# A gated scan with a router and eight experts: a new order for the last dozen units, seven of them gated by GpSimd and TensorE, two copies on VectorE, three fills held back

## The chip, the cores and the metric

The kernel runs on one core of one Trainium2 chip, as one launch. The metric is the device time of that launch in microseconds (us). The engines are TensorE (PE, and PEld for its weight loads), VectorE (DVE), ScalarE (ACT), GpSimd (POOL) and SyncE (SP), which here issues nearly all the transfers from one queue in the order of the program.

## The reference

All tensors are float32. A gated linear recurrence runs over 4 sequences of 5,056 tokens with 256 channels, and its output, as 20,224 tokens, goes to a mixture of 8 experts with one expert for each token and a capacity of 80.

```
log_a = 8 * sigmoid(r_gate) * log(clip(sigmoid(a_param)))
a_t   = exp(log_a);  norm = sqrt(max(1 - a_t*a_t, 1e-6))
x_g   = norm * sigmoid(i_gate) * x
h     = a_t * h + x_g          # one step for each token; y[t] = h
logits = y @ w_gate (256 x 8);  expert = argmax;  gate = its softmax
for each expert e (w1: 256 x 1024, w2: 1024 x 256):
    keep the 80 tokens with the highest gate
    out[kept] = gate * (relu(y[kept] @ w1[e]) @ w2[e])
every other row of out is 0
```

Only 640 of 20,224 rows of the output are not zero, so nearly the whole output is a fill with zeros.

## The kernel before, in words

**Units.** The tokens are cut into 40 units of 512 (the last has 256). For each unit three tiles of 512 KB are loaded (`Lr`, `Li`, `Lx`, line 120). The r gate is transposed by TensorE (`Tr`, line 128: eight matmuls of 128x128), ScalarE takes its tanh out of PSUM (`tr`, line 130) and the decay from it (`e`, line 142), GpSimd squares the decay (`q`, line 145) and ScalarE takes the root (`s`, line 148). ScalarE takes the tanh of the i gate (`ti`, line 152). The product (1 + tanh i) * x is made either on VectorE in one instruction (`v`, line 159) or on GpSimd in two (`u`, lines 156 and 157: add one, then multiply). TensorE transposes that product, half a unit at a time (`Tu`, line 164: four matmuls), VectorE multiplies it with the root in PSUM (`xg`, line 167) and runs the recurrence (`y`, line 175), both once for each half of the channels.

**Router.** After every four units TensorE makes logits (`G`, line 238); the steps `R0` to `R5`, with ten stages each, turn them into gates. Stage 0 copies 128x512 logits from PSUM (line 262, ScalarE), stages 2, 4 and 6 are VectorE's, stage 5 and 7 GpSimd's. After the last unit stand the rest of step 5, the merge (`M`) of the candidates, and a stretch of small instructions that picks 80 tokens for each expert (lines 484 to 539).

**Fills.** Row blocks of 512 tokens of the output are set to zero by SP (`Z`, line 230), 40 of them; all but the first are copied from the part of the output that is already zero (512 KB read, 512 KB written). They stand between the loads.

**Experts.** Each expert has a pair of halves. In a half, TensorE runs eight groups of two matmuls for the first product of expert e+1 and two for the second product of expert e (lines 629 and 631). When a half has been issued, SP loads that half's weights of the expert two further on (`load_w1`, line 381, and `load_w2`, line 384; 512 KB each) into the buffer just read. The first two experts' weights are loaded before (`W0` to `W7`), into slots of the big tile that the last units leave. GpSimd, ScalarE and VectorE gather the tokens' columns (lines 616 and 617). An indirect transfer on GpSimd's queue (line 649) writes the result of an expert to the output, and it may not run before the fills have landed.

**What sets the order.** `ORDER` is a list of tokens as named above, written out by hand or by a program. Each engine gets its instructions in this order, and SP its transfers. `SLOTS` says which of 50 slots of 512 KB holds each tile of each unit; a load waits until the slot's last reader is done, and everything behind it on SP's queue waits with it.

Of the kernel before, what the change touches and what calls it, by code (L numbers as in the profile page):

```python
# [13 lines left out]
ALU = mybir.AluOpType  # L14
# [14 lines left out]
SLOTS = dict(r=(14, 25, 30, 35, 38, 18, 21, 16, 34, 9, 11, 20, 13, 26, 25, 37, 42, 45, 40, 48, 41, 49, 22, 31, 24, 30, 44, 45, 41, 46, 49, 35, 32, 37, 42, 46, 44, 45, 41, 46),  # L29
             i=(34, 40, 4, 27, 37, 44, 23, 37, 28, 19, 15, 23, 32, 18, 46, 49, 38, 16, 21, 30, 28, 25, 26, 34, 37, 32, 43, 36, 38, 31, 36, 30, 41, 45, 36, 43, 49, 37, 38, 49),  # L30
             x=(20, 12, 29, 22, 40, 24, 6, 42, 36, 29, 27, 35, 41, 24, 36, 17, 29, 18, 27, 43, 33, 38, 47, 42, 33, 28, 32, 27, 34, 38, 33, 34, 48, 33, 38, 48, 40, 43, 40, 47),
             a=(15, 8, 31, 19, 33, 5, 14, 7, 17, 10, 30, 12, 28, 34, 14, 23, 35, 38, 19, 20, 27, 35, 23, 29, 25, 26, 40, 47, 28, 29, 43, 31, 40, 47, 34, 35, 36, 42, 48, 39))
# [32 lines left out]
    R5.4 Z R5.5 R5.6 R5.7 R5.8 F F F F F F F F M2 R5.9  # L65
"""
EARLY = 8


class Plan:  # L70

# [12 lines left out]
def moe_kernel(ctx, tc, x, r_gate, i_gate, a_param, w_gate, w1, w2, out, capacity=80):  # L84
# [75 lines left out]
    def u_transposes(u, h):  # L160
        pu = pus[u, h] = ps_u.tile([P, C], F32, name="pu")
        nb = ntok(u) // P
        for b in range(nb):
            nc.tensor.transpose(pu[:, b:nb * P:nb], tmb('x', u)[:, b, h * P:(h + 1) * P], ident)  # L164
# [556 lines left out]
```

## Time and profile before

| | |
|---|---|
| three runs | 292.08, 293.74 and 287.35 us, median 292.08 us |
| profiled execution | 287.59 us, of which the span is 285.9 us |
| busy: DVE, ACT, POOL, PE | 223.0, 232.9, 213.0, 211.1 us |
| moved by DMA | 100.74 MB, mean 352 GB/s |

The span runs from the first to the last instruction that the profiler recorded. Busy time is the time in which an engine had an instruction in work. Up to about 201 us the units run, to about 218 us the last router step and the picking of tokens, and then the experts.

### The profile page before, as it was taken

Reading aid. Unit: us, or ns where it says so; the run is one execution under the profiler, and the core shown is the slowest. Engines: PE = TensorE matmul, PEld = TensorE weight load, DVE = VectorE, ACT = ScalarE, POOL = GpSimd, SP = SyncE. Lnnn points to the kernel's source line nnn. Section 1 sums busy time; section 2 is a strip of 40 time slices with the busy share of each in tenths; the row PEclk is TensorE's granted clock in tenths of the full one; section 3 lists DMA queues with packets and bytes.
Section 4 is the critical chain, followed back from the end, with each engine's and each line's share of the span. In section 5 each row is a group of like instructions: output and inputs, shape, how many; then the busy total and the mean of one; then the engine's idle time right before and its main releaser. Section 6 shows DMA issues by size and latency. Waiting matters only on the chain.

```text
span 285.9 us, 5799 instructions
## 1 busy us (share of the span) xinstructions
PE 211.1 (74%) x1488; PEld 161.0 (56%) x1488; DVE 223.0 (78%) x506; ACT 232.9 (81%) x488; POOL 213.0 (75%) x372
## 2 busy tenths in 40 slices
PE   2635849598556985479857696486787889999995
PEld 2634723375444354462555325333676779999994
DVE  2018999999999999999999999999995663445510
ACT  7999999999999999999999999999264754544400
POOL 3279488789999999999999788998375682816521
PEclk9995977689959999779979997979999997999999
DMA  6999999999999999999889999999999997999831
GB/s 232 417 386 416 410 408 408 409 391 396 411 405 436 367 367 359 386 344 413 318 318 396 353 406 387 410 364 344 304 408 406 347 297 240 342 340 331 299 93 32
DMA packets 32825, 100.74 MB, mean 352 GB/s; under 512 B 3744, under 2 KB 12576, under 8 KB 32160
## 3 DMA queue, kind: packets, MB, share of 16 engines
q1 hardware_dynamic: 32400, 99.64, 93.1%
q0 software_dynamic: 384, 0.66, 0.7%
q8 instruction: 14, 0.23, 0.3%
q14 instruction: 27, 0.22, 0.2%
HBM read 99.10 MB, written 21.36 MB: 421 GB/s over the span
## 4 chain that ended last, share of the span: by engine, by line
DMA 29%; PE 21%; DVE 17%; POOL 12%; ACT 8%; issue 8%; SPq 2%; ACTq 1%; DVEq 0%; POOLq 0%
DMA Y<-in_x_dram 11%; PE po L631 9%; PE ph L629 7%; DVE Y L175 6%; POOL Y L157 6%; DMA Y<-in_i_gate_dram 6%; DMA Y<-in_r_gate_dram 6%; DMA Y<-in_moe_w_dram 4%; POOL Y L145 3%; DVE Y L159 3%; DMA Y<-in_moe_w_gate_dram 3%; DVE pu L167 3%; POOL Y L156 2%; ACT Y L142 2%; SPq L120 2%
## 5 line engine op out<-in xcount | busy, mean ns | idle before, releaser
L175 DVE TENSOR_TENSOR_SCAN Y<-Y,pu 128x512 f32<-128x512 f32 (+4 forms) x86 | 97.9, 1171 | 0.4
L164 PE MATMUL pu<-ident,Y 128*128 128x128 f32 x316 | 53.7, 303 | 49.0 <-DVE Y L175 26.0
L145 POOL TENSOR_TENSOR Y<-Y 128x1024 f32<-128x1024 f32 (+2 forms) x29 | 74.5, 2589 | 18.8 <-ACT Y L142 17.6
L164 PEld LDWEIGHTS pu<-ident,Y 128*128 128x128 f32 x316 | 38.7, 154 | 71.3 <-issue 37.9
L157 POOL TENSOR_TENSOR Y<-Y 128x1024 f32<-128x1024 f32 (+1 forms) x23 | 57.4, 2498 | 1.9
L128 PE MATMUL pr<-ident,Y 128*128 128x128 f32 x316 | 50.1, 313 | 11.5 <-DMA Y<-in_r_gate_dram 8.2
L128 PEld LDWEIGHTS pr<-ident,Y 128*128 128x128 f32 x316 | 43.5, 165 | 16.4 <-issue 6.7
L167 DVE SCALAR_TENSOR_TENSOR pu<-Y,pu 128x512 f32<-128x512 f32 (+1 forms) x80 | 51.2, 673 | 0.6 <-ACT Y L148 0.2
L142 ACT ACTIVATE Y<-Y,tiny 128x1024 f32<-128x1024 f32 (+2 forms) x48 | 49.5, 1089 | 0.1
L631 PE MATMUL po<-Y,rows 128*80 128x128 f32 x256 | 46.9, 279 | 0.0
L629 PE MATMUL ph<-Y 128*128 128x80 f32 x256 | 43.1, 263 | 2.7 <-DMA Y<-in_moe_w_dram 1.8
L629 PEld LDWEIGHTS ph<-Y 128*128 128x128 f32 x256 | 38.1, 196 | 3.4 <-POOL Y L617 3.3
L152 ACT ACTIVATE Y<-Y 128x1024 f32<-128x1024 f32 (+2 forms) x30 | 39.6, 1328 | 0.4 <-DMA Y<-in_i_gate_dram 0.3
L130 ACT ACTIVATE Y<-pr 128x1024 f32<-128x1024 f32 (+1 forms) x40 | 39.4, 1009 | 0.1
L616 ACT COPY Y<-Y 128x2 f32 x256 | 25.8, 191 | 16.7 <-issue 14.2
L148 ACT ACTIVATE Y<-Y 128x2048 f32<-128x2048 f32 (+2 forms) x26 | 37.5, 1493 | 0.4 <-POOL Y L145 0.2
L159 DVE SCALAR_TENSOR_TENSOR Y<-Y 128x1024 f32<-128x1024 f32 (+1 forms) x16 | 23.8, 1500 | 16.2 <-DMA Y<-in_moe_w_gate_dram 10.1
L617 POOL COPY Y<-Y 128x2 f32 x192 | 24.6, 195 | 14.7 <-DVE Y L646 5.7
L238 PE MATMUL pl<-Y 128*32 128x512 f32 x144 | 34.1, 1077 | 0.5 <-DVE Y L175 0.5
L156 POOL TENSOR_SCALAR Y<-Y 128x1024 f32<-128x1024 f32 (+1 forms) x23 | 26.6, 1158 | 6.0 <-ACT Y L152 5.7
L631 PEld LDWEIGHTS po<-Y,rows 128*80 128x80 f32 x256 | 29.2, 155 | 0.0
L643 DVE TENSOR_SCALAR rows<-ph 128x320 f32<-128x320 f32 x8 | 3.9, 492 | 27.1 <-PE ph L629 24.0
(165 smaller groups left out, 200.3 us busy)
## 6 DMA issues: line engine op xcount, KB each, us to landing
Y<-in_r_gate_dram SPq DMA_DIRECT2D x39, 512.0 KB, 6.9
Y<-in_i_gate_dram SPq DMA_DIRECT2D x39, 512.0 KB, 7.2
Y<-in_x_dram SPq DMA_DIRECT2D x39, 512.0 KB, 7.7
out_dram<-out_dram SPq DMA_DIRECT2D x38, 512.0 KB, 9.6
Y<-in_moe_w_dram SPq DMA_DIRECT2D x32, 512.0 KB, 6.9
out_dram<-Y SPq DMA_DIRECT2D x1, 512.0 KB, 10.4
Y<-in_x_dram SPq DMA_DIRECT2D x1, 256.0 KB, 5.7
Y<-in_i_gate_dram SPq DMA_DIRECT2D x1, 256.0 KB, 5.1
```

The lines of the kernel that those rows point to most:

```text
L128: nc.tensor.transpose(pr[:, h, b:nb * P:nb], rr[:, b, h * P:(h + 1) * P], ident)
L130: nc.scalar.activation(rslot(u), prs.pop(u)[:, :, :ntok(u)], AF.Tanh, scale=0.5)
L142: nc.scalar.activation(a[:, :, h], z[:, :, h], AF.Exp, scale=L[:, h:h + 1], bias=L[:, h:h + 1])
L145: nc.gpsimd.tensor_tensor(pair('r', u, m), a, a, op=ALU.mult)
L148: nc.scalar.activation(q, q, AF.Sqrt, scale=-0.25, bias=0.25)
L152: nc.scalar.activation(i, i, AF.Tanh, scale=0.5)
L157: nc.gpsimd.tensor_tensor(v, i, v, op=ALU.mult)
L164: nc.tensor.transpose(pu[:, b:nb * P:nb], tmb('x', u)[:, b, h * P:(h + 1) * P], ident)
L167: nc.vector.scalar_tensor_tensor(pu, rslot(u)[:, h], 0.5e-3, pu, op0=ALU.max, op1=ALU.mult)
L175: nc.vector.tensor_tensor_scan(y[:, s0:s1], a[:, s0:s1], q[:, s0:s1], init, op0=ALU.mult, op1=ALU.add)
L629: if e1 is not None: nc.tensor.matmul(ph[:, c % (FC // 2)], w1v(e1)[:, h, c * P:c * P + P], XG[:, e1, h], start=(h == 0), stop=(h == 1))
L631: if e2 is not None: nc.tensor.matmul(po[:, h, :P], h2T[:, c], w2v(e2)[:, c, h * P:h * P + P], start=(c == 0), stop=(c == FC - 1))
```

## The change

The list `ORDER` is the same up to its 471st token (in the units 26 and 27) and new from there, and the slots of 34 late tiles (from unit 27 on) are new. In the new part:

- Seven late units have a new kind of gating, `w`: GpSimd makes tanh(i) * x in place of tanh(i) with one instruction, and TensorE transposes both x and that product into the same PSUM tile, the second added to the first (eight matmuls for half a unit in place of four, four in place of two in the last unit). These are the units 30, 31, 32, 34, 36, 38 and 39. Before, 30, 32, 36, 38 and 39 were gated by GpSimd in two instructions, and 31 and 34 by VectorE. Units 33 and 37 stay with GpSimd in two instructions, 35 with VectorE.
- Stage 0 of the router steps 3 and 4 is a copy by VectorE, no longer by ScalarE.
- The last three fills (the very last is half as large) are taken out of the stretch before the experts. They are issued among the loads of the experts' weights, one after the first half of expert 2's `w1` and two after its second half.
- The loads `W0` to `W7` stand in another order, and those of the second product of expert 1 (`W6`, `W7`) stand behind eight more fills.
- The second round of the merge (line 354 and one `best`) is a token of its own, `M4`, and stands behind stage 2 of the last step.
- At the start GpSimd sets twelve single columns to zero and not six.

```
+    def times_tanh(u, m):
+        ti, v = flat_pair('i', u, m), flat_pair('x', u, m)
+        nc.gpsimd.tensor_tensor(ti, ti, v, op=ALU.mult)
     def u_transposes(u, h):
+        terms = [tmb(k, u) for k in ('xi' if u in plan.summed else 'x')]
         pu = pus[u, h] = ps_u.tile([P, C], F32, name="pu")
         nb = ntok(u) // P
         for b in range(nb):
-            nc.tensor.transpose(pu[:, b:nb * P:nb], tmb('x', u)[:, b, h * P:(h + 1) * P], ident)
+            for n, v in enumerate(terms):
+                nc.tensor.matmul(pu[:, b:nb * P:nb], v[:, b, h * P:(h + 1) * P], ident, start=(n == 0), stop=(n == len(terms) - 1), is_transpose=True)
...
-    for k in range(6): nc.gpsimd.memset(tiny[:, 70 + k % 4:71 + k % 4], 0.0)
+    for k in range(12): nc.gpsimd.memset(tiny[:, 70 + k % 4:71 + k % 4], 0.0)
...
         if s == LAST_STEP: nc.scalar.copy(lgs[s][:, HEAD:w], st['end'][:, :w - HEAD])
+        elif s >= 3: nc.vector.tensor_copy(lgs[s][:, :w], st['pl', s][:, :w])
         else: nc.scalar.copy(lgs[s][:, :w], st['pl', s][:, :w])
...
             find(0)
+        if n == 4:
             nc.vector.match_replace(cell, rows[:, NE:NE + 8], cell, -1.0)
             best(8)
...
+HELD = (1, 2)
...
-    zero_fill(-(-N // ZERO_TOKENS))
+    zero_fill(-(-(N - nz[0]) // ZERO_TOKENS) - sum(HELD))
+    filled = nz[0]
...
     def experts(arm):
+        nz[0] = filled
...
             if e1 is not None and e1 + 2 < E: load_w1(e1 + 2, half)
+            if e1 == 0: zero_fill(HELD[half])
             if e2 is not None and e2 + 2 < E: load_w2(e2 + 2, half)
...
-    R5.4 Z R5.5 R5.6 R5.7 R5.8 F F F F F F F F M2 R5.9
+    R5.3 Z R5.4 Z R5.5 R5.6 R5.7 R5.8 F F F F F F F F W6 W7 M2 R5.9
```

SP's queue, from the last load of a unit to the first weight loads of the experts' stage. Line 230 is a fill, 381 and 384 are halves of an expert's first and second weights (236, 389 and 392 in the changed kernel); the branch is the entry to the experts. Before:

```order
L230 DMA out_dram<-out_dram 16x8192 x8
L381 DMA Y<-in_moe_w_dram 128x2x512
L230 DMA out_dram<-out_dram 16x8192
L384 DMA Y<-in_moe_w_dram 128x4x256
L230 DMA out_dram<-out_dram 16x8192
L381 DMA Y<-in_moe_w_dram 128x2x512
L384 DMA Y<-in_moe_w_dram 128x4x256 x3
L230 DMA out_dram<-out_dram 16x8192 x2
L381 DMA Y<-in_moe_w_dram 128x2x512 x2
L230 DMA out_dram<-out_dram 16x8192 x8
L230 DMA out_dram<-out_dram 16x4096
L686 COMPARE_AND_BRANCH
```

The same stretch now, and on to the second load of expert 3:

```order
L236 DMA out_dram<-out_dram 16x8192 x6
L389 DMA Y<-in_moe_w_dram 128x2x512
L236 DMA out_dram<-out_dram 16x8192 x2
L392 DMA Y<-in_moe_w_dram 128x4x256 x2
L389 DMA Y<-in_moe_w_dram 128x2x512 x2
L236 DMA out_dram<-out_dram 16x8192 x8
L392 DMA Y<-in_moe_w_dram 128x4x256 x2
L236 DMA out_dram<-out_dram 16x8192 x3
L697 COMPARE_AND_BRANCH
L236 DMA out_dram<-out_dram 16x8192
L236 DMA out_dram<-out_dram 16x4096
```

Two fills and one half fill moved from before the branch to behind it, where they stand after the first halves of expert 2 and ahead of expert 3; before the branch three whole fills stand behind the last weights.

VectorE, units 32 to 35, where the router's step 3 begins (line 281 is its stage 2). Lines 159, 167 and 175 are the gating, the product with the root and the scan. Before:

```order
L167 SCALAR_TENSOR_TENSOR pu<-Y,pu 128x512 x2
L175 SCALAR_TENSOR_TENSOR Y<-Y,pu 128x512
L159 SCALAR_TENSOR_TENSOR Y<-Y 128x1024
L175 SCALAR_TENSOR_TENSOR Y<-Y,pu 128x512
L281 TENSOR_REDUCE Y<-pl 128x32
L282 TENSOR_TENSOR pl<-pl,Y 128x16x16
```

Now (lines 160, 173 and 181; 268 is the copy of the logits):

```order
L268 COPY lg<-pl 128x512
L173 SCALAR_TENSOR_TENSOR pu<-Y,pu 128x512 x2
L181 SCALAR_TENSOR_TENSOR Y<-Y,pu 128x512
L288 TENSOR_REDUCE Y<-pl 128x32
L289 TENSOR_TENSOR pl<-pl,Y 128x16x16
L160 SCALAR_TENSOR_TENSOR Y<-Y 128x1024
```

VectorE has a copy of 128x512 where a gating product of 128x1024 stood; of three such products in this part of the program one is left, and there are two copies.

TensorE, from the logits of the last full group to the last logits of all (line 164 transposes the product, 128 the r gate, 238 makes logits, 266 turns them). Before:

```order
L266 MATMUL pl<-ident,lg 128x128 x4
L128 MATMUL pr<-ident,Y 128x128 x4
L164 MATMUL pu<-ident,Y 128x128 x8
L238 MATMUL pr<-Y 32x256 x8
L164 MATMUL pu<-ident,Y 128x128 x4
L238 MATMUL pr<-Y 32x128 x8
```

Now:

```order
L273 MATMUL pl<-ident,lg 128x128 x4
L129 MATMUL pr<-ident,Y 128x128 x4
L170 MATMUL pu<-ident,Y 128x128 x16
L244 MATMUL pr<-Y 32x256 x8
L170 MATMUL pu<-ident,Y 128x128 x8
L244 MATMUL pr<-Y 32x128 x8
```

The last two units need 24 matmuls for their transposes and not 12.

## Rows read from the trace of the kernel before

**Rows 1.** Busy time by stage; the first row names the columns.

```profile
core 0: us, PE busy (x) PEld busy (x) DVE busy (x) ACT busy (x) POOL busy (x), PEclk, DMA share, GB/s
140.00:150.00 10.00, 5.95 (x38) 5.16 (x38) 9.90 (x15) 9.97 (x10) 9.92 (x7) 0.83 0.76 255
150.00:190.00 40.00, 28.60 (x171) 15.71 (x170) 39.83 (x55) 39.83 (x42) 35.14 (x26) 0.91 1.00 381
190.00:201.00 11.00, 6.89 (x60) 3.71 (x58) 10.66 (x19) 9.35 (x14) 8.90 (x16) 1.00 1.02 371
201.00:218.00 17.00, 13.37 (x102) 11.13 (x102) 15.57 (x58) 7.68 (x36) 10.06 (x32) 1.00 1.01 366
238.00:240.00 2.00, 2.00 (x12) 2.00 (x12) 0.42 (x4) 0.00 (x0) 0.00 (x0) 0.50 0.93 323
241.00:281.00 40.00, 40.00 (x395) 40.00 (x394) 15.43 (x109) 16.59 (x150) 18.89 (x103) 1.00 0.77 256
```

**Rows 2.** Chain of work that ended last, experts: start, us, what.

```profile
225.67 10.57 DMA Y<-in_moe_w_dram
...
280.53 1.79 PE bank L682 x16
```

**Rows 3.** TensorE's instructions in order of time, around the second expert.

```profile
234.20 0.39 PE L631 MATMUL po<-Y,rows 128*80 128x128 f32 x2
236.38 0.42 PE L629 MATMUL ph<-Y 128*128 128x80 f32 x2 [1.79 <-DMA Y<-in_moe_w_dram]
```

**Rows 4.** SP's issues: first of expert 2's loads, then one at each half.

```profile
225.67 5.86 SPq L381 DMA_DIRECT2D Y<-in_moe_w_dram  x3
...
241.28 0.37 SPq L381 DMA_DIRECT2D Y<-in_moe_w_dram  x1
...
244.52 0.37 SPq L381 DMA_DIRECT2D Y<-in_moe_w_dram  x1
```

**Rows 5.** Late units, 140 to 202 us, by form: busy, mean ns, idle before.

```profile
L167 DVE SCALAR_TENSOR_TENSOR pu<-Y,pu 128x512 f32<-128x512 f32 x26 | 16.6, 681 | 0.2 <-ACT Y L148 0.2
L159 DVE SCALAR_TENSOR_TENSOR Y<-Y 128x1024 f32<-128x1024 f32 x3 | 3.8, 1270 | 0.0
...
L262 ACT COPY lg<-pl 128x512 f32<-128x512 f32 x2 | 1.1, 573 | 0.0
...
L157 POOL TENSOR_TENSOR Y<-Y 128x1024 f32<-128x1024 f32 x8 | 19.0, 2381 | 0.7
...
L156 POOL TENSOR_SCALAR Y<-Y 128x1024 f32<-128x1024 f32 x7 | 7.4, 1054 | 0.2
```

**Rows 6.** VectorE in order of time: first and last instruction of the merge's second round.

```profile
201.98 0.08 DVE L354 MATCH_VALUE_LOAD Y<-rows,Y 128x8 f32 x1
...
202.57 0.18 DVE L341 FIND_INDEX8 Y<-rows,Y 128x8 uint32<-128x32 f32 x1
```

**Rows 7.** GpSimd at the start: the single columns by form, and its first square.

```profile
L214 POOL MEMSET tiny<- 128x1 f32 x6 | 0.3, 88 | 0.0
...
9.90 1.89 POOL L145 TENSOR_TENSOR Y<-Y 128x1024 f32<-128x1024 f32 x1 [7.02 <-ACT Y L142]
```

**Rows 8.** SP's issues ahead of the experts: the last fills.

```profile
211.42 12.57 SPq L230 DMA_DIRECT2D out_dram<-out_dram  x9
```

**Rows 9.** Transfers issued 225.6 to 226.2 us, then 234.8 to 236: KB, us to landing.

```profile
Y<-in_moe_w_dram SPq DMA_DIRECT2D x1, 512.0 KB, 10.6
...
Y<-in_moe_w_dram SPq DMA_DIRECT2D x1, 512.0 KB, 9.0
```

**Rows 10.** The chain of work that ended last, in the late units.

```profile
185.99 3.81 PE pl L238 x16
189.80 1.02 PE pu L164 x8
...
191.91 2.35 POOL Y L157
```

**Rows 11.** Waits: who waited for whom, us in total, times, longest.

```profile
POOL out_dram L649 <- DMA Y<-in_moe_w_dram: 5.1, 1, 5.1
```

More of the change, by code (lines that the diff above doesn't have):

```diff
@@ L66 @@
+    R5.3 Z R5.4 Z R5.5 R5.6 R5.7 R5.8 F F F F F F F F W6 W7 M2 R5.9
 """
 EARLY = 8
+HELD = (1, 2)
 class Plan:
@@ L77, in __init__ @@
             self.order.append((kind, *map(int, filter(None, token[len(kind):].split(".")))))
-        self.by_pool = {u + k for kind, *a in self.order if kind == 'u' for u in a[:1] for k in range(a[1])}
+        self.by_pool, self.summed = ({u + k for kind, *a in self.order if kind == g for u in a[:1] for k in range(a[1])} for g in 'uw')
         self.steps = STEPS
@@ L159, in gated, with times_tanh @@
             nc.vector.scalar_tensor_tensor(v, i, 1.0, v, op0=ALU.add, op1=ALU.mult)
+    def times_tanh(u, m):
+        ti, v = flat_pair('i', u, m), flat_pair('x', u, m)
+        nc.gpsimd.tensor_tensor(ti, ti, v, op=ALU.mult)
     def u_transposes(u, h):
+        terms = [tmb(k, u) for k in ('xi' if u in plan.summed else 'x')]
         pu = pus[u, h] = ps_u.tile([P, C], F32, name="pu")
@@ L163, in u_transposes @@
         for b in range(nb):
-            nc.tensor.transpose(pu[:, b:nb * P:nb], tmb('x', u)[:, b, h * P:(h + 1) * P], ident)
+            for n, v in enumerate(terms):
+                nc.tensor.matmul(pu[:, b:nb * P:nb], v[:, b, h * P:(h + 1) * P], ident, start=(n == 0), stop=(n == len(terms) - 1), is_transpose=True)
     def normed(u, h):
@@ L213, in moe_kernel @@
     warm = tiny[:, 21:22]
-    for k in range(6): nc.gpsimd.memset(tiny[:, 70 + k % 4:71 + k % 4], 0.0)
+    for k in range(12): nc.gpsimd.memset(tiny[:, 70 + k % 4:71 + k % 4], 0.0)
     dio = tiny[:, 4:20]
@@ L261, in r_copy @@
         if s == LAST_STEP: nc.scalar.copy(lgs[s][:, HEAD:w], st['end'][:, :w - HEAD])
+        elif s >= 3: nc.vector.tensor_copy(lgs[s][:, :w], st['pl', s][:, :w])
         else: nc.scalar.copy(lgs[s][:, :w], st['pl', s][:, :w])
@@ L353, in merge @@
             find(0)
+        if n == 4:
             nc.vector.match_replace(cell, rows[:, NE:NE + 8], cell, -1.0)
@@ L406, in moe_kernel @@
     ps_t = tstack.enter_context(tc.tile_pool(name="ps_t", bufs=1, space=bass.MemoryType.PSUM))
-    zero_fill(-(-N // ZERO_TOKENS))
+    zero_fill(-(-(N - nz[0]) // ZERO_TOKENS) - sum(HELD))
+    filled = nz[0]
     KG, KF = -(-CAP // 8) * 8, 14
@@ L588, in experts @@
     def experts(arm):
+        nz[0] = filled
         fstack = ExitStack()
@@ L639, in products @@
             if e1 is not None and e1 + 2 < E: load_w1(e1 + 2, half)
+            if e1 == 0: zero_fill(HELD[half])
             if e2 is not None and e2 + 2 < E: load_w2(e2 + 2, half)
```

29 lines of the change are left out of this document (14 added, 15 removed).

## The prediction, made before the changed kernel ran

> **What bounds the kernel now.** I read the busy time by stage first [rows 1], since the limits change along the program. In the late units, 150 to 201 us, VectorE is busy 39.83 of 40 us and then 10.66 of 11, ScalarE 39.83 of 40 and then 9.35 of 11, and the transfers fill their engines (share 1.00 and 1.02). GpSimd has 4.9 us free in the first of these stretches and TensorE 11.4. So three resources are full there at once, and the reader should see that relief of one is worth only what the next of them lets through. From 201 to 218 us VectorE leads with 15.57 of 17 us.
>
> The chain of waits comes second, for the experts [rows 2]. Its longest link is a transfer: the first weights of expert 2 were issued at 225.67 us and the chain stands on them for 10.57 us. TensorE's own rows show what of this hurt [rows 3]: its last product before ended at 234.20 + 0.39 = 234.59 us, and it stood still for 1.79 us. The granted clock then was 0.50 (its lower level, 1.2 GHz) at 238 to 240 us [rows 1]. SP issues a load when a half has been issued, so its times mark the halves [rows 4]: the half that began at 236.38 us ended at 241.28, 4.90 us, and the next, at full clock, took 244.52 - 241.28 = 3.24. The stall has therefore cost 1.79 + (4.90 - 3.24) = 3.45 us. From 241 to 281 us TensorE is busy 40.00 of 40 at a clock of 1.00, and its last product ends by 280.53 us [rows 1, 2]: past the stall the experts are TensorE's alone, and a microsecond saved before them, if they are fed, is a microsecond of the total.
>
> **The change, part by part.** The sum is made against the profiled execution, 287.59 us (span 285.9). The median of the runs shown, 292.08 us, stands 1.6% above it.
>
> VectorE in the late units: two gating products of 128x1024 go (units 31 and 34), 2 x 1.27 = 2.54 us [rows 5]. Two copies of 128x512 out of PSUM come, for which VectorE has no row. Nearest from below is ScalarE's copy of the same shape and source, 0.573 us; from above VectorE's own product of that size in PSUM, with one more input, 0.681. I take 0.62, nearer to neither, which gives 1.24. Net -1.3 us (ends -1.18 and -1.39). VectorE is full, so this is on the path.
>
> ScalarE loses the two copies, 2 x 0.573 = 1.15 us, in the same full stretch. So it follows VectorE's gain nearly to the end.
>
> GpSimd: the second instruction, 1.05 us, goes for units 30, 32, 36 and 38 and half of it for 39, some 4.7 us; the multiply of units 31 and 34 comes, 2 x 2.38 = 4.8 [rows 5]. Net zero, beside 4.9 us of idle time [rows 1]. For one unit the result is ready 1.05 us earlier.
>
> TensorE: six units with 8 more matmuls and one with 4, together 52. Eight took 1.02 us on the chain [rows 10], so 52 x 0.1275 = 6.6 us at that clock. Cover: 11.4 us of idle time from 150 to 190 and 4.1 to 201 us [rows 1]. I take zero on the path; without cover it is 6.6 us, and 13.3 at half clock (the second rival). A tile of the i gate is now held until TensorE has read it, so the load that takes its slot, and SP's queue behind it, may be later by the half microsecond of a half unit's four more matmuls. It is covered as long as fills wait in the queues (share 1.00).
>
> The merge's second round, 201.98 to 202.75 us, so 0.77 us [rows 6], now follows stage 2 of the last step, where stage 4 waits behind it. In return stage 4 of step 4 leaves the scans and takes the place in which VectorE waited for the last logits. Between -0.8 and +0.8 us; I take zero, since VectorE does the same work up to the end of both. The six more columns cost 6 x 0.088 = 0.5 us on GpSimd, which then waits 7.02 us for ScalarE [rows 7]: nothing.
>
> The held fills: behind them stood expert 2's first weights. A fill of 0.524 MB at the 366 GB/s of 201 to 218 us is 1.43 us [rows 1], and SP, kept back by its earlier transfers, needed 12.57 / 9 = 1.40 for each [rows 8]. Two and a half are 3.6 us. These weights landed at 225.67 + 10.6 = 236.3 us [rows 9] and now would at 232.7. They are wanted at 234.59 - 1.3 = 233.3. So the stall is gone by a margin of 0.6 us: -3.45 us. `W6` and `W7`, moved behind eight fills, still stand ahead of these weights, and are wanted in the same moment.
>
> What is late next: the held fills stand in front of expert 3's `w1` and expert 2's `w2`. Their last piece was issued at about 234.8 us and landed 9.0 us later, at 243.8 [rows 9]; the bytes ahead of it are the same as before. TensorE wants it in the second half of its next step: 234.59 + 6.48 + 3.24 - 1.3 = 243.0 us. So 0.8 us is given back.
>
> Sum: -1.3 - 3.45 + 0.8 = -3.9 us, hence **283.7 us**.
>
> **The rivals.**
>
> *The wait only moves (0.20).* The trace has the transfers full from 150 to 218 us [rows 1] and 9.0 us from issue to landing in the middle of the expert stage [rows 9]. If expert 3's weights land later than reckoned, the stall of 3.45 us comes back one expert further on, low clock included, and VectorE's gain is lost in it or not: 286.3 to 287.6 us. For it speaks that no byte is saved; against it that the GB/s fall to 256 from 241 us on, so there is room soon after. The Trainium skill, "DMA: Bandwidth & Descriptors", Queues, rings and completion order, says that each of the 16 engines takes descriptors in the order of its ring. By that, weights queued behind a held fill cannot pass it, and this rival's 287 us is what it would give. The long 10.6 us behind the fills [rows 9] agree with it; whether the second expert has the margin no row before shows.
>
> *TensorE becomes the bound, slower (0.12).* On the chain from 185.99 to 191.9 us TensorE already has the last word: logits 3.81, transposes 1.02 us [rows 10]. If the 52 matmuls all lie on the path, the total is 287.6 - 1.3 - 3.45 + 6.6 = 289.4 us; at the lower clock, which a longer pause brought in rows 1, 13.3 in place of 6.6 gives 296.1. It decides from 4.8 us on the path upwards (3.45 + 1.3), which is 38 of the 52 at full clock. Against it: 15.5 us of idle time before 201 us, and GpSimd's result, for which TensorE waits on that same chain (2.35 us), comes 1.05 us earlier.
>
> *The stage itself gets shorter (0.20).* The new order and slots also reach the loads from unit 28 on, issued about 140 us. There the transfers fell to a share of 0.76, 2.4 us of 10 unused [rows 1]. If the new slots close that gap, the data of expert 3 are no longer late and the scans may be earlier: -1.3 - 3.45 - 2.4 = -7.1 us at most, without the gap but with no give-back -4.75. That is 280.5 to 282.8 us. Against it: VectorE is 99% busy even in that gap (9.90 of 10), so only the transfers gain.
>
> GpSimd's first write of results waited 5.1 us for transfers [rows 11], and the gathers of expert 4 stand behind it. With fills in flight later this wait may grow by 1 to 2 us; those gathers are wanted a whole expert, 6.5 us, later, so I count nothing.
>
> **How the numbers follow.** Forecast 0.48 at 283.7 us; the wait moves 0.20; TensorE binds 0.12; the stage gets shorter 0.20. The range: its lower end is the full gain of the last rival, 280. Its upper end takes in the moved wait (287.6), the cheap form of the second (289.4), and the forecast in a run that stands as far above the profiled one as the median did: 283.7 x 1.016 = 288.2. So 280 to 290; outside are the dear forms of the second rival and a moved wait in such a run, together under 0.2. About 2% is what a measurement of this kernel can tell from no change, since its three runs lie 2.2% apart. Against 287.6 us, faster by over 2% means under 281.8: most of the last rival and an eighth of the forecast, 0.23. Against the median of 292.08 it means under 286.2, which the forecast and the last rival reach unless their own runs stand higher, some 0.5. Between the two I take faster 0.36, within 2% 0.55, slower 0.09, the last from TensorE as the bound.
>
> **What would show it.** In the new profile: VectorE still above 99% busy to the end of the scans, which end 1 to 1.5 us before 201; two rows of VectorE copies of 128x512 at 0.57 to 0.68 us; transposes with 16 matmuls and no idle time of VectorE behind them. No wait of TensorE for weights at the second expert, and a clock of 1.00 through it; a wait under 1 us at the next one. The forecast is wrong if TensorE's wait for transfers stands at the third expert with 1.8 us or more, if VectorE's idle time before the end of the scans grows by over 2 us, or if TensorE's last product ends no earlier than at 280.5 us.

## The result, and the profile after

The changed kernel takes 289.41 us (median of 20 runs, 287.61 to 292.99), the kernel before on the same chips 289.19 us (20 runs, 286.25 to 294.71). The comparison, which leaves disturbed runs of either out, gives a ratio of 1.0074 with a 95% interval of 1.005 to 1.0097: slower by 0.7%, some 2 us, where 283.7 us was forecast. The profiled execution took 287.84 us (span 286.1).

Busy time by stage of the changed kernel, the columns as in [rows 1]:

```profile
core 0: us, PE busy (x) PEld busy (x) DVE busy (x) ACT busy (x) POOL busy (x), PEclk, DMA share, GB/s
140.00:150.00 10.00, 6.82 (x43) 5.86 (x42) 9.90 (x16) 9.95 (x11) 9.92 (x7) 0.83 0.87 340
150.00:190.00 40.00, 33.60 (x202) 22.11 (x203) 38.67 (x53) 38.98 (x40) 36.08 (x25) 0.87 0.93 343
190.00:201.00 11.00, 8.11 (x72) 5.16 (x71) 8.52 (x12) 7.53 (x10) 6.38 (x9) 1.00 1.01 350
201.00:218.00 17.00, 13.35 (x85) 11.86 (x86) 15.83 (x58) 8.07 (x34) 9.70 (x34) 0.90 1.03 362
238.00:240.00 2.00, 2.00 (x22) 2.00 (x21) 1.78 (x17) 1.25 (x14) 1.08 (x9) 1.00 0.99 387
241.00:281.00 40.00, 39.56 (x389) 39.44 (x389) 15.61 (x114) 16.55 (x150) 19.15 (x103) 1.00 0.85 291
```

Look at VectorE's column (DVE). It had 39.83 of 40 and 10.66 of 11 us [rows 1]; now it has 38.67 and 8.52. From 190 to 201 us ScalarE and GpSimd have become emptier together with it (TensorE has not: 8.11 us, after 6.89), so these three wait for something that has to be found. The same columns from the end of unit 24's scans, up to which both orders are the same, to the end of the last scan, in the kernel before and then in the changed one:

```profile
138.16:200.98 62.82, 43.27 (x281) 26.42 (x279) 62.10 (x88) 60.99 (x66) 55.72 (x48) 0.92 0.97 365
138.02:202.89 64.87, 50.51 (x333) 35.11 (x331) 60.85 (x86) 60.29 (x64) 54.59 (x41) 0.89 0.93 340
```

VectorE's busy time fell by 1.25 us, and its idle time grew from 62.82 - 62.10 = 0.72 to 64.87 - 60.85 = 4.02 us. A growth of over 2 us was one of the signs by which the forecast would be wrong. The experts show the opposite: at 238 to 240 us TensorE does 22 matmuls, not 12, and the clock is 1.00, not 0.50.

The experts, in order of time: the one wait of TensorE for a transfer (in brackets), then two links of the chain that ended last.

```profile
244.96 0.42 PE L641 MATMUL po<-Y,rows 128*80 128x128 f32 x2 [0.44 <-DMA Y<-in_moe_w_dram]
```

```profile
234.72 10.10 DMA Y<-in_moe_w_dram
280.80 1.79 PE bank L693 x16
```

The stall of [rows 3] is gone, and what is late next costs 0.44 us. Expert 2's first weights land 8.7 us after their issue, not 10.6 [rows 9]. Yet the last group of products begins at 280.80 us, no sooner than the 280.53 of [rows 2]. What the experts gained was lost ahead of them, and three instants show where (the end of the scans is the last scan's start and duration; the experts run from their first product to that last group):

| profiled execution | scans end | from there to first product | experts |
|---|---|---|---|
| before, 287.59 us | 201.0 | 22.7 | 56.9 |
| after, 287.84 us | 202.9 (+1.9) | 23.9 (+1.2) | 54.0 (-2.8) |

Where the first loss comes from is read on SP's queue. SP's issues of the changed kernel, 181 to 190 us; start, duration, what:

```profile
181.47 0.33 SPq L121 DMA_DIRECT2D Y<-in_r_gate_dram  x1
187.34 0.33 SPq L121 DMA_DIRECT2D Y<-in_x_dram  x1
187.71 0.70 SPq L236 DMA_DIRECT2D out_dram<-out_dram  x1
188.52 0.52 SPq L121 DMA_DIRECT2D Y<-in_x_dram  x1
189.48 0.33 SPq L121 DMA_DIRECT2D Y<-in_i_gate_dram  x1
```

and the same loads in the kernel before:

```profile
182.83 0.33 SPq L120 DMA_DIRECT2D Y<-in_i_gate_dram  x1
...
185.47 0.33 SPq L120 DMA_DIRECT2D Y<-in_x_dram  x1
```

GpSimd's instruction ahead of the load at 187.34:

```profile
184.92 2.39 POOL L158 TENSOR_TENSOR Y<-Y 128x1024 f32<-128x1024 f32 x1 [0.36 <-DMA Y<-in_x_dram]
```

In the changed kernel the load at 187.34 is `Lx38`. It goes into slot 43, which GpSimd's second instruction of unit 37 reads until then (184.92 + 2.39 = 187.31 us), and SP stands still for it (5.0 us), with the loads of the last unit, `Lx39` and `Li39`, behind. So `Li39` goes out at 189.48 us, where the kernel before issued it at 182.83. It lands 5.7 us later. What that does is a row on each engine, with its idle time in brackets (ScalarE, GpSimd, VectorE):

```profile
195.28 1.28 ACT L153 ACT_TABLE_LOAD   x1 [3.18 <-DMA Y<-in_i_gate_dram]
...
197.28 1.26 POOL L163 TENSOR_TENSOR Y<-Y 128x512 f32<-128x512 f32 x1 [3.95 <-ACT Y L153]
...
200.84 0.76 DVE L173 SCALAR_TENSOR_TENSOR pu<-Y,pu 128x256 f32<-128x256 f32 x2 [2.21 <-ACT Y L149]
201.51 1.38 DVE L181 TENSOR_TENSOR_SCAN Y<-Y,pu 128x256 f32<-128x256 f32 x2
```

The second loss is in the last step. VectorE, stage 2 of step 5 (line 288), the merge's second round (first instruction 362), stage 4 (line 307):

```profile
205.28 0.29 DVE L288 TENSOR_REDUCE Y<-pr 112x16 f32<-112x128 f32 x1 [0.26 <-PE pr L273]
205.61 0.29 DVE L289 TENSOR_TENSOR Y<-pr,Y 112x128 f32<-112x128 f32 x1
205.82 0.08 DVE L362 MATCH_VALUE_LOAD Y<-rows,Y 128x8 f32 x1
...
206.96 0.28 DVE L307 SCALAR_TENSOR_TENSOR Y<-Y,tiny 112x128 f32<-112x128 f32 x1
```

The kernel before: TensorE turns the last logits, then VectorE's stages 2 and 4.

```profile
202.11 0.70 PE L266 MATMUL pr<-ident,Y 128*112 128x128 f32 x4
203.23 0.28 DVE L281 TENSOR_REDUCE Y<-pr 112x16 f32<-112x128 f32 x1
203.87 0.44 DVE L300 SCALAR_TENSOR_TENSOR Y<-Y,tiny 112x128 f32<-112x128 f32 x1
```

Stage 4 begins 206.96 - 205.28 = 1.68 us after stage 2; in the kernel before it was 0.64 (203.23 to 203.87), because the merge's round ran at 201.98 us [rows 6], while TensorE was still turning the logits (to 202.81 us) that stage 2 needs.

The form rows that the sum rested on, as in [rows 5]:

```profile
L268 DVE COPY lg<-pl 128x512 f32<-128x512 f32 x2 | 1.4, 692 | 0.4 <-PE pl L244 0.4
L160 DVE SCALAR_TENSOR_TENSOR Y<-Y 128x1024 f32<-128x1024 f32 x1 | 1.2, 1215 | 0.0
```

### The profile page after: what moved, and what is told of

It reads as the page before. It is cut to its first block, busy times and chain, and to the rows that moved or that the text cites. A ratio compares the mean times of both kernels' runs of the same rounds, so it can differ in the third digit from the quotient of the medians.

```text
span 286.1 us, 5901 instructions
## 1 busy us (share of the span) xinstructions
PE 220.6 (77%) x1540; PEld 173.2 (61%) x1540; DVE 222.8 (78%) x506; ACT 232.1 (81%) x486; POOL 213.1 (74%) x375
## 4 chain that ended last, share of the span: by engine, by line
PE 26%; DMA 20%; DVE 16%; POOL 14%; issue 11%; ACT 9%; SPq 2%; ACTq 1%; POOLq 0%; DVEq 0%
PE po L641 8%; PE ph L639 7%; POOL Y L146 7%; DMA Y<-in_x_dram 5%; DVE Y L181 5%; DMA Y<-in_i_gate_dram 5%; DVE pu L173 4%; PE pl L244 4%; DMA Y<-in_moe_w_dram 4%; DMA Y<-in_moe_w_gate_dram 3%; POOL Y L158 3%; DMA out_dram<-out_dram 3%; PE pu L170 2%; PE pr L129 2%; POOL Y L157 2%
## 5 line engine op out<-in xcount | busy, mean ns | idle before, releaser
L170 PE MATMUL pu<-ident,Y 128*128 128x128 f32 x368 | 60.3, 303 | 44.5 <-DVE Y L181 22.1
L170 PEld LDWEIGHTS pu<-ident,Y 128*128 128x128 f32 x368 | 46.1, 156 | 65.7 <-issue 33.8
L129 PE MATMUL pr<-ident,Y 128*128 128x128 f32 x316 | 54.5, 335 | 8.8 <-DMA Y<-in_r_gate_dram 7.5
L129 PEld LDWEIGHTS pr<-ident,Y 128*128 128x128 f32 x316 | 48.1, 178 | 12.6 <-issue 5.7
L158 POOL TENSOR_TENSOR Y<-Y 128x1024 f32<-128x1024 f32 x18 | 46.6, 2590 | 1.8 <-DMA Y<-in_x_dram 0.4
L641 PE MATMUL po<-Y,rows 128*80 128x128 f32 x256 | 45.8, 274 | 0.4 <-DMA Y<-in_moe_w_dram 0.4
L639 PEld LDWEIGHTS ph<-Y 128*128 128x128 f32 x256 | 37.1, 191 | 1.5 <-POOL Y L627 1.3
L627 POOL COPY Y<-Y 128x2 f32 x192 | 24.8, 197 | 13.4 <-issue 5.1
L160 DVE SCALAR_TENSOR_TENSOR Y<-Y 128x1024 f32<-128x1024 f32 (+1 forms) x14 | 21.6, 1557 | 15.7 <-DMA Y<-in_moe_w_gate_dram 10.0
L157 POOL TENSOR_SCALAR Y<-Y 128x1024 f32<-128x1024 f32 x18 | 21.8, 1210 | 5.8 <-ACT Y L153 5.6
L627 DVE COPY Y<-Y 128x2 f32 x192 | 20.3, 176 | 5.1 <-issue 5.1
```

What stands on the lines that cost most here:

```text
L129: nc.tensor.transpose(pr[:, h, b:nb * P:nb], rr[:, b, h * P:(h + 1) * P], ident)
L158: nc.gpsimd.tensor_tensor(v, i, v, op=ALU.mult)
L170: nc.tensor.matmul(pu[:, b:nb * P:nb], v[:, b, h * P:(h + 1) * P], ident, start=(n == 0), stop=(n == len(terms) - 1), is_transpose=True)
L627: else: eng.tensor_copy(dst, src)
L639: if e1 is not None: nc.tensor.matmul(ph[:, c % (FC // 2)], w1v(e1)[:, h, c * P:c * P + P], XG[:, e1, h], start=(h == 0), stop=(h == 1))
L641: if e2 is not None: nc.tensor.matmul(po[:, h, :P], h2T[:, c], w2v(e2)[:, c, h * P:h * P + P], start=(c == 0), stop=(c == FC - 1))
```

## The experiments

Theory: the held fills do what was forecast; the loss is the new order and the new slots, through SP's queue, and the last step's order. Rivals: TensorE's further matmuls; VectorE or ScalarE as a bound that I misjudged; the granted clock. All profiles were read in the same three parts. Ratios are to the kernel before on the same chip, since chips differ. The column "last three units" is the time from the end of unit 36's scans to the end of all.

| run | median (range), us | ratio, 95% | profiled | scans end | last three units | to first product | experts |
|---|---|---|---|---|---|---|---|
| e1 | 285.92 (284.18-289.37) | 0.996 [0.990, 1.002] | 284.18 | 201.3 | 10.9 | 22.7 | 53.2 |
| e2 | 293.55 (291.87-295.71) | 1.027 [1.021, 1.033] | 295.48 | 204.1 | 13.1 | 24.0 | 60.4 |
| e3 | 290.63 (290.17-291.74) | 1.016 [1.012, 1.020] | 290.51 | 201.8 | 12.6 | 23.4 | 56.4 |
| e4 | 289.59 (288.04-290.65) | 1.012 [1.007, 1.016] | 290.65 | 204.0 | 13.0 | 23.2 | 56.4 |
| e5 | 294.46 (291.76-295.66) | 1.026 [1.016, 1.035] | 291.76 | 204.2 | 11.9 | 23.4 | 57.1 |
| e6 | 292.05 (289.71-292.34) | 1.014 [1.004, 1.024] | 291.78 | 206.8 | 14.9 | 23.7 | 53.2 |
| e7 | 289.33 (288.32-293.04) | 1.004 [0.999, 1.010] | 290.72 | 204.9 | 11.7 | 23.8 | 53.2 |
| e9 | 285.65 (283.8-290.21) | 0.996 [0.993, 1.000] | 289.12 | 205.3 | 10.9 | 23.7 | 53.2 |
| e10 | 288.45 (286.04-289.77) | 1.009 [1.006, 1.012] | 286.04 | 203.1 | 11.1 | 22.7 | 53.2 |
| e11 | 288.54 (286.4-290.5) | 1.011 [1.006, 1.017] | 287.36 | 204.5 | 10.7 | 22.7 | 53.2 |
| e12 (as e1) | 288.39 (285.23-289.94) | 1.010 [1.006, 1.014] | 285.23 | 202.4 | 10.7 | 22.7 | 53.2 |
| e13 | 289.22 (288.03-292.28) | 1.016 [1.008, 1.024] | 288.03 | 201.2 | 11.2 | 25.2 | 53.2 |
| e14 | 289.92 (288.47-293.19) | 1.014 [1.009, 1.018] | 293.19 | 204.6 | 14.4 | 23.2 | 56.4 |
| before, four profiles | | | 285.75-289.29 | 201.0-202.0 | 10.7-10.8 | 22.7-23.2 | 54.7-57.0 |
| after, three profiles | | | 287.84-288.27 | 202.9-203.9 | 13.5-14.2 | 23.9-24.8 | 53.2-54.0 |

The three parts leave out the end, from the last group of products to the end of the span. It takes 5.2 to 5.4 us in 15 of the 20 profiles, but 6.3 in e6, 6.8 in e13, 7.1 in e7, 7.2 in e3 and 7.3 in e14. Why is open; the totals of these five hold 1 to 2 us that none of the three parts shows.

**e1: the held fills alone**, in the kernel before; e12 is the same kernel on another chip.

```
+HELD = (1, 2)
+            if e1 == 0: zero_fill(HELD[half])
```

> The kernel before, with the last three fills held back until expert 2's first weights are in the queue, and nothing else of the change. Theory (the held fills are worth what the prediction said, and the new late order loses it again): no wait of TensorE for weights at the second expert, granted clock 1.00 from 234 to 241 us, the experts some 2.8 us shorter than before (first product 223.7 us as before, last product end 277 to 278), total 2.5 to 3.5 us under the kernel before. Rival (the experts became shorter in the changed kernel only because they began 3.1 us later, when the transfers had caught up): the wait of 1.8 us stays or moves one expert on, total within 1 us of before.

> The kernel before with the held fills and nothing else, once more, as the measure for the three cuts on this chip and to see whether it beats both kernels. Theory (the fills held back are worth the stall at the second expert's weights and the low clock behind it, 3.3 us in the profiles): 2 to 4 us under the kernel before, and under the changed kernel's 287.6 to 290. Rival (the low clock comes in some executions wherever it finds a pause, and takes back what the fills give): under 1 us.

The experts take 53.2 us in both, 3.7 less than in the first profile of before, without a wait for weights and at a clock of 1.00. In the times it is 0.4% faster on one chip, which its interval does not tell from no change, and 1.0% slower on the other: the fills' gain is sure in the profile and not in the total.

**e2: the changed kernel without the held fills.**

```
-HELD = (1, 2)
+HELD = (0, 0)
```

> The changed kernel with its three last fills ahead of the experts again, the new late order kept. Theory: the late units and the last router step end as in the changed kernel (first product of the experts at about 226.8 us), and the stall at the second expert is back, though smaller since the experts start 3 us later than before: 1 to 3.5 us above the changed kernel. Rival (the held fills do nothing once the experts start late): as the changed kernel, within 0.7 us.

More than expected: TensorE waits 3.9 us for expert 2's weights, then works at half clock, and the experts take 60.4 us. Without the held fills the changed kernel is 2.7% slower than before, with them 0.7%, so within it they are worth some 2% (4.1 us by the medians, which are of different chips).

**e3: the load cured.**

```
-    ... xg36.0 Lx38 tr38 e38.1 Z s37.1 y36.1 q38.1 G8 Lx39 Tu37.0 ... R4.1 Li39 Z ...
+    ... xg36.0 Lx39 Li39 Lx38 tr38 e38.1 Z s37.1 y36.1 q38.1 G8 Tu37.0 ... R4.1 Z ...
```

> The changed kernel with two of its last loads (x and i gate of unit 39) issued ahead of the x load of unit 38, which waits for GpSimd's second instruction of unit 37 to free its slot. Theory (SP's queue stood behind that slot, and ScalarE then waited 3.2 us for unit 39's i tile): that load is issued at about 185.5 us and not 189.5, ScalarE's wait falls under 1 us, VectorE's wait of 2.2 us before its last product with the root goes, the scans end 1.8 to 2.4 us earlier (about 200.8 us) and so does all that follows. Total 1.5 to 2.5 us under the changed kernel. Rival (TensorE's doubled transposes, or the transfers themselves, set the end of the units): the tile arrives earlier, the scans end within 0.7 us of where they did.

ScalarE's wait is gone, and the scans end at 201.8 us. That part of the theory holds, though the last three units still take 12.6 us: now GpSimd stands for `Lx38` itself, before unit 38's product (SP's issue of `Li39`, ScalarE without a wait, GpSimd).

```profile
185.31 0.33 SPq L121 DMA_DIRECT2D Y<-in_i_gate_dram  x1
191.94 1.28 ACT L153 ACT_TABLE_LOAD   x1
192.47 3.57 POOL L163 TENSOR_TENSOR Y<-Y 128x1024 f32<-128x1024 f32 x2 [1.64 <-DMA Y<-in_x_dram]
```

The total did not follow, because the experts took 56.4 us, 2.4 more than in the changed kernel's first profile, and the end 1.9 more. TensorE's clock, by stretches of e3 (columns as before):

```profile
226.00:228.00 2.00, 2.00 (x18) 1.89 (x16) 1.26 (x11) 1.06 (x12) 1.83 (x16) 0.93 1.13 264
228.00:230.00 2.00, 2.00 (x11) 2.00 (x11) 1.64 (x15) 2.00 (x21) 0.83 (x7) 0.50 1.11 442
230.00:232.00 2.00, 2.00 (x12) 2.00 (x12) 0.82 (x6) 0.46 (x5) 1.83 (x15) 0.50 0.87 370
```

In the changed kernel these stretches stand at 1.00; its fall came at 203 to 208 us, where VectorE waits 0.26 us for TensorE (the row at 205.28).

**e4: the last router steps where they stood before.**

```
-... e39.1 w39.1 ... y39.0 R4.3 ... R5.0 R4.4 R4.5 R4.6 M0 R5.1 ... R5.2 Z Z R4.8 M1 M4 M3
+... e39.1 R4.3 w39.1 ... y38.0 R4.4 ... R5.0 R4.5 R4.6 M0 M4 R5.1 ... R4.8 M1 M3 R5.2
```

> The changed kernel with the router's step 4 (exponential and stage 4) ahead of the last scans and the merge's second round ahead of the last step's stage 2, as in the kernel before. Theory: from the end of the scans to the experts' first product 22.7 us as before and not 23.9, since 0.8 us of the merge and 1.0 us of stage 4 no longer stand in the last step's chain while VectorE sits idle before the last scans: 0.8 to 1.2 us under the changed kernel. Rival (VectorE has the same work in either order): within 0.4 us.

The last step took 23.2 us, 0.7 less than in the changed kernel's first profile, and the scans end at 204.0 (204.1 in e2, 202.9 to 203.9 in the changed kernel). The clock again fell in the first expert, and nothing was won.

**e5: the gating back**, in the changed kernel (`w` to `u` or `v` for all seven units).

> The changed kernel, with the gating of the seven late units back in its old form (five on GpSimd, two on VectorE, TensorE transposes one tile); new order, new slots, VectorE's two copies and the held fills stay. Theory (the new order of the loads, not the gating, makes the scans end 1.9 us late; the gating only moved 2 x 1.27 us off VectorE, which stands idle for 3.8 us there anyway): the scans end between 202.5 and 204.5, and the time is 0 to 1.5 us above the changed kernel's. Rival A (the 52 further matmuls of TensorE set the pace of the late units): the scans end 1 us or more sooner than in the changed kernel, and the time falls by 1 us or more. Rival B (VectorE is the bound as I forecast): the full 2.5 us more.

The scans end inside the theory's range, but the median is 5.0 us above the changed kernel's on another chip (ratios 1.026 and 1.007): more than any theory had. In the profile 3.1 us of it or more is the second expert again (57.1 us: a wait of 2.0 us for weights, half clock behind it). Rival A is out: fewer matmuls did not help. For the scans, as far as one profile tells, rival B is out too: from the end of unit 24's scans VectorE has 3.3 us more of work than in the changed kernel (64.17 us busy, after 60.85), and the last scan ends only 0.3 to 1.1 us later (65.6 us, after 64.9, 65.3 and 64.5 in the three profiles). Most of what the new gating takes off VectorE comes back as idle time.

**e6: the new gating alone**, for units 30, 36, 38, 39, beside the held fills in the old order.

> The kernel before with the held fills, and the new gating on units 30, 36, 38 and 39 alone, in the old order and slots (these four were GpSimd's before too, so VectorE's work stays the same). Theory (the gating is neutral where the order is kept): the time is within 0.7 us of the kernel before with the held fills alone, some 284 to 286.5 us. Rival A (TensorE's further matmuls cost): 1 to 2 us above that. Rival B (GpSimd's shorter product shortens the chain into the scans): 1 us or more below it.

This fell: the scans end at 206.8 us, not 201.3. Of these 5.5 us, 1.4 were there by 111 us, ahead of the first changed unit. The units up to 36 take as long as in e1 (39.8 us from the same scan on); the last three take 14.9, not 10.9. SP's longest wait from 182 to 192 us (engine, for whom: us in total, times, longest) shows why, and then the two loads of unit 39:

```profile
SPq L121 <- PE pu L170: 6.8, 1, 6.8
```

```profile
187.93 0.33 SPq L121 DMA_DIRECT2D Y<-in_i_gate_dram  x1
188.30 0.52 SPq L236 DMA_DIRECT2D out_dram<-out_dram  x1
188.93 0.50 SPq L121 DMA_DIRECT2D Y<-in_r_gate_dram  x1
```

`Li39` waits for a slot until TensorE has transposed, and goes out at 187.93 us; in e1 at 183.51. Behind it on the queue stands `Lx38`: it goes out at 189.89 us, not 186.40, lands 5.6 us later, and GpSimd's product of unit 38, which needs it, begins at 195.64 us after 3.05 us of idle time (in e1 GpSimd takes up unit 38 at 191.22).

```profile
189.89 0.33 SPq L121 DMA_DIRECT2D Y<-in_x_dram  x1
195.64 3.58 POOL L163 TENSOR_TENSOR Y<-Y 128x1024 f32<-128x1024 f32 x2 [3.05 <-issue]
```

That is the term that I had at nothing: a tile held until TensorE has read it holds SP's queue.

**e7: VectorE's copies alone**, beside the held fills in the old order.

```
+        elif s >= 3: nc.vector.tensor_copy(lgs[s][:, :w], st['pl', s][:, :w])
```

> The kernel before with the held fills, and the logits of the last router steps copied by VectorE and not by ScalarE, in the old order. Theory (VectorE bounds the late units in the old order, idle for 0.5 of 51 us): two to three copies of 0.69 us lengthen the way to the end of the scans by 1.2 to 2 us over the kernel before with the held fills alone. Rival (ScalarE is as much the bound, and 0.58 us less on it for each copy makes up for it): within 0.4 us of it.

The scans end 2.4 to 3.6 us later than in e12 and e1, the last three units take 0.8 to 0.9 us longer. In the times it stands between e1 and e12 (1.004), so a price of the copies is not shown.

**e9, e10, e11: work taken off VectorE, off ScalarE, off both**, in the kernel of e1 (ScalarE's cut first, then VectorE's).

```
+        if m == 1 and u in (31, 34): i = i[:, :P]
...
+            if u in (31, 34): i, v = i[:, :P], v[:, :P]
```

> The kernel before with the held fills, and of VectorE's two gating products (units 31 and 34) only 128 of 1024 columns; the rest of both is left out of the computation. This takes some 2 us of work off VectorE, more than the change did, and leaves order, slots and loads as they are. Theory A, that of my prediction (VectorE is full and its time is on the path): the scans end 1.5 to 2 us sooner than at 201.3, so 199.3 to 199.8. Theory B (the loads, and ScalarE behind them, set the pace of the late units; VectorE is only just kept busy): 0 to 0.5 us sooner, VectorE's idle time from 150 us to the end of the scans grows from 0.4 to 2 us or more.

> The kernel before with the held fills, and of ScalarE's tanh of the i gates of units 31 and 34 only 128 of 1024 columns; the rest of both is left out of the computation. This takes some 1.9 us of work off ScalarE and nothing off VectorE. Theory A (VectorE bounds): the scans end within 0.3 us of 201.3, since VectorE was idle for 0.4 us. Theory B (ScalarE behind the loads bounds, with VectorE as full): within 0.5 us too. Rival (ScalarE alone is the bound): 1 us or more sooner, which VectorE's full stretch should forbid.

> The kernel before with the held fills, with both cuts: VectorE's gating products and ScalarE's tanh of units 31 and 34 on 128 of 1024 columns, the rest left out of the computation. If two full engines bound together, this gives 1.5 to 2 us where each alone gave less than 0.5. If the loads (the slots, freed by VectorE, TensorE and GpSimd, and the transfers at a share of 1.0) bound, it gives less than 1 us as well. By theory A it equals the cut on VectorE alone, 1.5 to 2 us.

The times of e9 are 2.7 us under e12's by the median, on the same chip, which speaks for theory A. Its profile, of an execution (289.12 us) above most of its runs, speaks against it: the scans end at 205.3 us, 2.9 later than in e12, and the saving was lost at once. VectorE and GpSimd in that execution:

```profile
171.22 3.45 DVE L161 SCALAR_TENSOR_TENSOR Y<-Y 128x128 f32<-128x128 f32 x1
```

```profile
170.92 3.60 POOL L146 TENSOR_TENSOR Y<-Y 128x2048 f32<-128x2048 f32 x1 [1.16 <-DMA Y<-in_r_gate_dram]
```

The same cut product took 0.27 us at 158.25. Here it began 0.3 us after GpSimd's square and ended with it (174.67 and 174.52 us). In e12 the whole product had begun 0.07 us ahead of that square:

```profile
170.86 1.20 DVE L160 SCALAR_TENSOR_TENSOR Y<-Y 128x1024 f32<-128x1024 f32 x1
170.93 4.60 POOL L146 TENSOR_TENSOR Y<-Y 128x2048 f32<-128x2048 f32 x1 [1.16 <-DMA Y<-in_r_gate_dram]
```

Beginning 0.4 us later had put it behind GpSimd's instruction. Cutting ScalarE as well (e11, same collision at 158.98 us, 3.41 us) gave nothing, though e9's cut is part of it; cutting ScalarE alone (e10) nothing either, as expected. So theory A is neither shown nor ruled out.

**e13 and e14: e3 with more idle products (`F`) on TensorE, whose edit stands here; and e3's and e4's edits together.**

```
-... M1 M4 M3 Z F F F F F F F F F I1 ... R5.8 F F F F F F F F W6 ...
+... M1 M4 M3 Z F F F F F F F F F F F F F F F F F F F F F I1 ... R5.8 F F F F F F F F F F F F W6 ...
```

> The changed kernel with the loads of unit 39 ahead of the x load of unit 38 (as in e3), and with 16 more idle products of 128x128 on TensorE in its pauses of the last router step, 12 before the pause of 1.64 us and 4 at the end. Theory (in e3 the load was cured and the scans ended 1.2 us sooner, but the granted clock of 0.50 at 227 to 235 us took it back): the clock stays at 1.00 through the first expert, the experts take 53.5 to 54.5 us and not 56.4, and the time is 1.5 to 3 us under e3's, some 287.5 to 289. Rival (the clock falls there whatever TensorE did in the pause): experts at 56 us again, the time as e3's or above.

> The changed kernel with both repairs: the loads of unit 39 ahead of the x load of unit 38, and the places of the last router steps as in the kernel before (four of its steps). Gating, slots, VectorE's copies and the held fills stay. Theory (the late end of the scans is the load's, the late end of the last step the order of the router's): scans end at 201.5 to 202.5, the first expert's product 22.7 to 23.2 us later, and without a low clock in the experts 285.5 to 287.5 us; with one as in e3 and e4, 289 to 290.5. Rival (the two repairs hit the same wait): no sooner than e3.

In e13 the clock holds through the experts (53.2 us) and the scans end at 201.2, both as the theory has it, but it fell to 0.59 and 0.55 at 220 to 224 us instead, and the last step took 25.2 us. The fall of the clock was moved, not avoided. e14 has the shorter last step (23.2), but in its profile, of its slowest run (293.19), the last three units take 14.4 us and the clock falls in the first expert; its quickest run took 288.47. So the two repairs together were not better than either. The scans are late there by waits of VectorE of 1.18 and 0.95 us ahead of unit 38's products, behind a wait of GpSimd of 1.57 us for `Lx38` and a clock of 0.57 from 196 to 200 us; which of the two did it is open.

**e8, e15, e16: the kernel before again; e17, e18: the changed kernel again.**

> The kernel before as it is, for a second profile of it. Its runs fall into two groups some 4 us apart. Theory: the stall of TensorE at the second expert's weights and the low clock behind it come in every execution, so this profile shows them again, and a wait of 1 to 2.5 us for the DMA at the first products of the second expert. Rival: they come in some executions alone, and this one may show neither (then the held fills are worth less in the median than the 3.3 us of the profiles).

> The kernel before as it is, for a further profile. Theory (its quick executions, 284.4 to 286.5, have no stall at the second expert's weights, and the two profiles at 287.6 and 289.3 show slower ones): a profile under 286.8 us shows a wait under 0.5 us at the second expert, or no low clock behind it. Rival (the stall is in every execution, and quick ones gain elsewhere, by the clock in the late units): a wait of 1.5 us or more, with a clock of 0.5 behind it, at 286 us too.

> The kernel before as it is, once more, with the same two expectations as the run ahead of it: under 286.8 us either no wait over 0.5 us at the second expert's weights (theory), or a wait of 1.5 us or more with a clock of 0.5 behind it (rival).

> The changed kernel as it is, for a second profile of it, since four profiles of the kernel before spread by 1.0 us at the end of the scans (201.0 to 202.0) and by 0.5 us in the last step (22.7 to 23.2). Theory (the x load of unit 38 holds up the i tile of unit 39 in every execution, and the merge's second round stands in front of stage 4): ScalarE waits 2.5 us or more for the i tile of unit 39, the scans end at 202.5 to 204, the first product of the first expert stands 23.5 to 24.2 us behind that, and no wait over 0.6 us for weights at the second expert. Rival (the late end was that execution's low clock): the scans end at 201 to 202, without the wait.

> The changed kernel as it is, for a third profile, with the same expectations as the run ahead of it: a wait of ScalarE of 2.5 us or more for the i tile of unit 39 and scans that end at 202.5 to 204 (theory), or 201 to 202 without it (rival).

Both expectations on the kernel before were half right. The stall is in every execution: 1.79, 2.0, 1.3 and 1.7 us. The low clock behind it is not. The quickest profile (285.75 us), TensorE's wait and the same stretch as in [rows 1]:

```profile
236.32 0.42 PE L629 MATMUL ph<-Y 128*128 128x80 f32 x2 [1.69 <-DMA Y<-in_moe_w_dram]
```

```profile
238.00:240.00 2.00, 2.00 (x22) 2.00 (x21) 0.52 (x5) 0.33 (x1) 0.00 (x0) 1.00 0.91 317
```

With the low clock the experts take 56.9 and 57.0 us, without it 54.7 and 55.1. So the held fills' gain is 3.7 us in some executions and 1.5 to 1.9 in others, against e1's 53.2.

The changed kernel repeats itself: ScalarE waits for `Li39` in each profile,

```profile
196.25 1.28 ACT L153 ACT_TABLE_LOAD   x1 [3.63 <-DMA Y<-in_i_gate_dram]
```

```profile
195.64 1.28 ACT L153 ACT_TABLE_LOAD   x1 [3.31 <-DMA Y<-in_i_gate_dram]
```

(e17, e18), and the scans end at 203.9 and 203.3.

## Why the prediction was wrong

Over four profiles of before and three of after, the means differ by 203.3 - 201.5 = +1.8 us at the end of the scans, 24.2 - 22.8 = +1.4 in the last step, and 53.5 - 55.9 = -2.4 in the experts: +0.8 together, where -3.9 was forecast. That 289.41 us lies inside the range of 280 to 290, and that within 2% was the likeliest outcome (0.55), is luck: the upper end was there for a wait that only moves and for matmuls at their full price, and neither came. Point by point:

- **Held fills, -3.45 + 0.8.** Right in the mechanism: no stall at the second expert, the clock at 1.00, a small wait at the third (0.44 us, then none in the two further profiles). The size was that of executions with the low clock; against the mean of four the two terms together are -2.4, not -2.65. I took one execution's clock for a property of the kernel.
- **VectorE, -1.3, "VectorE is full, so this is on the path": failed.** Its work fell as forecast (products of 128x1024 from 3.8 to 1.2 us, copies of 0.69 us where I took 0.62), but not the time. Its idle time from the end of unit 24's scans to the last scan is 0.7 to 1.6 us in the four profiles of before and 3.5 to 4.4 in the three of after. Up to the end of unit 36's scans the changed kernel is ahead by 1.3 us: 189.0, 189.7, 189.8 against 190.2, 191.2, 191.3, 190.3. But 0.9 of it only moved: the top eight of the router's step 3 (0.93 us) stood ahead of these scans and now stand behind them, as the two kernels' rows show.

```profile
185.76 0.40 DVE L333 MAX8 Y<-rows 128x8 f32<-128x256 f32 x1
188.91 0.40 DVE L340 MAX8 Y<-rows 128x8 f32<-128x256 f32 x1
```

- **The failed step behind it: loads and slots at nothing, "covered as long as fills wait in the queues".** From unit 36 on the changed kernel takes 13.5 to 14.2 us, the kernel before 10.7 to 10.8: +3.1. VectorE's work there grew by the top eight (0.9) and a copy (0.7) and lost stage 4 (0.9); its idle time went from 0.3 to between 2.2 and 2.9 us. I had looked at whether transfers were short of bytes (the share of 1.00) and not at which load stands at the head of SP's queue. `Lx38` waited there 5.0 us for GpSimd, with the last unit's loads behind it, and `Li39` went out 6.6 us later than in the kernel before. e3 gives 4.2 of this back and ends the scans 1.1 to 2.1 us sooner. The other 2.4 us of `Li39` are, in e3, a wait for the slot that TensorE still reads, the form that the sentence named and that I had put at half a microsecond; e6 shows it without the new order, at 6.8 us of SP. With the order of e3 VectorE's idle time from unit 36 on is 1.4 us (e3), 0.1 (e13) and 2.4 (e14): the cure is not sure, and no run got the lost time back in its total. The last unit has no later work to hide behind.
- **The merge, between -0.8 and +0.8, taken as zero.** Stage 4 of step 4 left the scans and took VectorE's pause, as said, which puts 0.9 us behind the scans that was inside them; the merge's round then came out of the pause and onto the path. The last step grew by 1.4 us in the mean, and e4 got 1.0 of it back. With the 0.9 that left the scans the net is some +0.5: inside the bounds, on the wrong side of zero.
- **TensorE, 52 matmuls at nothing.** Their time was covered: VectorE waits for transposes for 0.2 us in the first profile and 1.0 in the second. The rival of TensorE as the bound came true in another way than by its price: not through the matmuls' time but through what they hold (e6).
- **GpSimd, nothing.** So it was, 3.95 us of waiting behind ScalarE included.
- **The stage itself gets shorter, a rival.** The share of the transfers from 140 to 150 us did rise, from 0.76 to 0.87, and the scans end later all the same.

What stays open: why the held fills alone are 1.0% slower on one chip. Five of the six runs of e12 lie above its profiled one and were not profiled. Likewise which of the executions have a low clock, and when, is described here and not explained. No kernel tried beats the kernel before with certainty.

## What to carry to other kernels

Where one in-order queue issues all loads, price a new order or new buffers by walking that queue: for each of the last loads, who frees its slot, when, and what stands behind it. Time saved on an engine with a busy share near 1 can come back as idle time at the next late load, as VectorE's did here; look at the last two or three pieces of work, which nothing covers. And take more than one profile of the kernel before: a stall that is always there may cost half as much in the next execution.

## What the hardware showed that I had not expected

- A product of VectorE with two tiles of SBUF and a product of GpSimd exclude each other: 0.27 us alone, 3.45 and 3.41 us when GpSimd's 3.60 us square had begun 0.3 us before. It goes the other way too: in e12 GpSimd's square took 4.60 us where VectorE's product of 1.20 us had begun just ahead of it. The Trainium skill, "SBUF — State Buffer", Who interferes with whom, says that a VectorE instruction with two SBUF inputs contends with a GpSimd instruction that reads SBUF, over shared ports that are an exclusive lock; these rows agree. The profile shows the blocked time as busy time, with no wait in brackets, so a full VectorE can hold some of it. VectorE's products with one operand in PSUM show no such thing: 26 of 128x512 take at most 0.70 us each in the changed kernel and in e9.
- TensorE's clock fell to its lower level (0.50) in every profile between 175 and 179 us, and later at places that differ: 203 to 208 (after), 227 to 235 (e3), 242 to 250 (e2), 220 to 224 (e13), or nowhere before the last products (e1). In the experts a fall goes with 1.8 to 3.2 us (56.9 and 57.0 against 54.7 and 55.1 in the kernel before; 56.4 in e3, e4 and e14 against 53.2), so a change of 1 us ahead can move the total by more than itself.
